# Strided mask and identity in one first transfer, fewer warm-up products, masks put by ScalarE, merged mix_t, strided sums behind the adds, and u^T's transfers on SyncE: a fused sparse-attention and low-rank/channel mixer kernel

## The chip, the cores and the metric

The kernel runs on one core of a Trainium2 chip. The core has five engines that work side by side, each through its own list of instructions in order: TensorE (PE in the profile; PEld is its weight load), VectorE (DVE), ScalarE (ACT), GpSimd (POOL) and SyncE (SP, which here only issues DMAs). They wait for one another by semaphores. Sixteen DMA engines move data between the main memory (HBM) and the on-chip memory (SBUF); TensorE writes its sums into a small memory of eight banks (PSUM). The metric is the device time of one execution in microseconds (us).

## What is computed

Attention over 8 batches, 8 heads, 576 positions and 64 channels, with two kinds of masks, and then a mixer. Cut to what matters:

```python
# q, k, v: (8, 8, 576, 64)
scores = np.matmul(q, k.transpose(0, 1, 3, 2)) / 8
pos = np.arange(576); rel = pos[:, None] - pos[None, :]
mask_local = (rel >= 0) & (rel < 32)                       # heads 0 to 3
mask_strided = (rel >= 0) & (pos[None, :] % 32 == pos[:, None] % 32)   # heads 4 to 7
attn = softmax(np.where(mask, scores, -1e9)) @ v
x = attn.transpose(0, 2, 1, 3).reshape(8, 576, 512)
h = x.transpose(0, 2, 1) @ U @ V                           # U (576, 32), V (32, 576): mixes positions
u = x + h.transpose(0, 2, 1)
out = u + np.maximum(u @ w_ch1, 0) @ w_ch2                 # w_ch1 (512, 2048), w_ch2 (2048, 512)
```

U, V and the two weight matrices come as 64-bit floats, and are converted on the chip. Products that must be exact are made of a high and a low part (`uh` and `ul`, `gh` and `gl`, two parts of each weight), three products in place of one.

## The kernel before, in words

**Blocks.** The channel mixer runs in nine blocks n = 0 to 8: one for the first 512 positions of each batch, and a last one for the eight tails of 64 positions. A block goes through 16 chunks `fc` of 128 hidden units. `gemm1` (line 648) makes 12 products of 128x512 for a chunk, ScalarE makes `gh` from it (line 652), VectorE `gl` (line 653), and `gemm2` (line 665) adds 12 more products into four banks `acc`. gemm2 runs one chunk behind gemm1. At a block's end `split` (lines 637 to 640) makes the next block's `uh` (ScalarE) and `ul` (VectorE) from `raw`, the transposed u, and `finish` (line 672) adds `acc` to u and stores it; the next block's gemm2 waits for these adds, since it writes the same banks.

**Attention beside it.** While block n runs, the attention of batch n + 1 is put between its products, a step at a time: `advance` hands out the steps of `attention` by half chunks ("slots", 32 a block) at rates that A_EARLY, A_LATE and A_TAIL give. For batches 2 to 7: the two pairs of local heads (`local_pairs`: scores, softmax, transposes, outputs), then the strided heads' results are copied in, `mix_t` makes x^T U in two halves of 256 channels (lines 514 and 518), `mix_u` adds V's product (lines 537 and 539), `mix_tail` does the 64 positions at the end, and `transposes` turns u by VectorE (line 619) and by 32 small DMAs into `raw` (line 624), half of them issued by ScalarE and half by SyncE. The strided heads of these batches are not done on TensorE: GpSimd multiplies (lines 442 and 470) and VectorE sums (lines 444 and 472), at a rate that S0 and S1 set by slots.

**The prefix.** The batches 0 and 1 are done at the start, all eight pairs of heads (`early_pair`, in the order 2, 3, 0, 1 of the pairs of each batch: strided pairs first). Their positions are sorted so that the strided mask becomes a band as the local one is. `quarter` then makes u^T of batch 0, a quarter of the channels for each pair. Scores begin with two products that put the mask into PSUM (line 340: an identity times the mask), on which the products of q and k are added (line 346); then maximum and difference (VectorE, lines 356 and 357), exponential (ScalarE, line 361), transposes (line 368, with the identity `ident`), a copy (line 371) and the outputs (line 381). In front of the first and of the second scores stand eight products of zeros each (line 338, WARM), to keep TensorE busy. SyncE loads q, k and v first, then weights; GpSimd issues the strided mask, the local mask with the 16-bit identity, and `ident`.

**Weights.** In block 0 the weights are still being converted (lines 129 to 132, 205 and 206: ScalarE and VectorE), each load gated by a one-word copy on GpSimd (line 169) behind a due exponential.

**Order.** A scheduler sets each engine's list from the order in which the code is written, readiness by its own estimate, and hints `issue_after`. `psx2` gives the two banks `px` (in the prefix `acc` as well), one user at a time.

## Time and profile before

| what | value |
|---|---|
| median of 3 runs (lowest, highest) | 927.82 us (927.54, 929.11) |
| the profiled execution's own time | 928.37 us |
| its span, first to last instruction | 926.1 us |
| mean granted TensorE clock | 0.991 |
| HBM read, written | 54.14 MB, 11.67 MB |
| DMA packets | 39036, 75.29 MB |

The page cuts the span into 40 slices of 23 us, with one digit per slice: the busy share in tenths (9 is 90% or more), and for the clock the tenths of full speed that TensorE was granted.

```profile
PE   7899989999999999999999999999999999999997
DVE  4579996665886588658765786667863341122111
POOL 1223493343853393429433764356530000000000
PEclk9899999999999999999999999999999999999999
DMA  9869313201230125011500141014200230001001
```

VectorE's digits are high in the third to sixth slice, which is block 0, and the DMA's in the first three. POOL's work ends with the strided heads of batch 7.

### The profile page before, as it was taken

The page shows a single profiled execution, that of the slowest core. Times are in us where ns is not written, and L with a number is a line of the kernel's source. Part 1 is how long each engine was busy: PE and PEld are TensorE (multiplying, and loading weights), DVE is VectorE, ACT ScalarE, POOL GpSimd, SP SyncE. Part 2 cuts the span into 40 slices and gives each one's busy share as a digit, 9 for nine tenths or more (in the row PEclk, how much of TensorE's full clock was granted, in tenths as well). Part 3 has the DMA queues.
Part 4 walks back from the last instruction along what each step waited for, and adds up shares of the span by engine and source line. Part 5 has one row for each costly group of instructions (what it writes and reads, how often), then busy time and mean ns, then how long its engine had stood idle before and what let it go on. Part 6 is the DMA issues. An engine that isn't in the chain of part 4 may idle for free.

```text
span 926.1 us, 16819 instructions
## 1 busy us (share of the span) xinstructions
PE 902.6 (97%) x6997; PEld 718.0 (78%) x6998; DVE 548.6 (59%) x895; ACT 244.2 (26%) x478; POOL 338.4 (37%) x378
## 2 busy tenths in 40 slices
PE   7899989999999999999999999999999999999997
PEld 4667767777887788778877787778877888888885
DVE  4579996665886588658765786667863341122111
ACT  3457522142123312331224121422142111121110
POOL 1223493343853393429433764356530000000000
PEclk9899999999999999999999999999999999999999
DMA  9869313201230125011500141014200230001001
GB/s 352 299 205 357 117 54 107 73 2 52 76 145 2 52 55 178 1 52 33 181 8 18 50 168 50 1 53 148 73 1 1 57 120 17 1 1 46 0 1 46
DMA packets 39036, 75.29 MB, mean 81 GB/s; under 512 B 6464, under 2 KB 22864, under 8 KB 37040
## 3 DMA queue, kind: packets, MB, share of 16 engines
q1 hardware_dynamic: 27312, 66.87, 20.7%
q10 hardware_dynamic: 10560, 4.73, 2.0%
q0 software_dynamic: 1088, 2.62, 0.8%
q8 instruction: 55, 0.90, 0.4%
q14 instruction: 21, 0.17, 0.1%
HBM read 54.14 MB, written 11.67 MB: 71 GB/s over the span
## 4 chain that ended last, share of the span: by engine, by line
PE 84%; DVE 4%; DMA 2%; POOL 1%; issue 1%; ACT 0%; SPq 0%; DVEq 0%; ACTq 0%; POOLq 0%
PE acc L665 40%; PE ph L648 39%; PE px L381 1%; DMA w<-in_w_dram 1%; PE px L346 1%; DVE cv L132 1%; DVE s_st L444 1%; PE px L368 1%; PE px L514 1%; DMA od<-x 1%; PE px L537 1%; DMA st<-in_strided_dram 1%; DVE w L206 1%; POOL tmp L442 1%; DVE gl L653 0%
## 5 line engine op out<-in xcount | busy, mean ns | idle before, releaser
L653 DVE SCALAR_TENSOR_TENSOR gl<-ph,gh 128x512 fp32r<-128x512 f32 x144 | 98.9, 688 | 230.1 <-ACT gh L652 229.4
L648 PE MATMUL ph<-uh,w 128*128 128x512 f32 x648 | 215.9, 394 | 0.0
L652 ACT ACTIVATE gh<-ph 128x512 fp32r<-128x512 f32 x144 | 86.2, 599 | 476.9 <-PE ph L648 400.8
L470 POOL TENSOR_TENSOR tmp<-st,s_st 128x448 f32<-128x448 f32 (+7 forms) x162 | 137.3, 876 | 190.8 <-DVE st L472 106.8
L442 POOL TENSOR_TENSOR tmp<-st 128x576 f32<-128x576 f32 (+6 forms) x162 | 175.0, 1121 | 76.5 <-DMA st<-in_strided_dram 66.6
L665 PE MATMUL acc<-w,gh 128*128 128x512 f32 x648 | 196.8, 391 | 0.0
L648 PEld LDWEIGHTS ph<-uh,w 128*128 128x128 f32 x648 | 121.9, 189 | 26.8
L665 PEld LDWEIGHTS acc<-w,gh 128*128 128x128 f32 x648 | 121.3, 188 | 25.6
L472 DVE TENSOR_REDUCE st<-tmp 128x64 f32<-128x64 f32 (+8 forms) x162 | 136.3, 878 | 7.8 <-POOL tmp L470 7.0
L648 PE MATMUL ph<-ul,w 128*128 128x512 f32 x324 | 126.8, 391 | 0.0
L665 PE MATMUL acc<-w,gl 128*128 128x512 f32 x324 | 121.6, 392 | 4.1 <-DVE gl L653 4.1
L444 DVE TENSOR_REDUCE s_st<-tmp 128x9 f32<-128x576 f32 (+6 forms) x162 | 87.2, 563 | 17.5 <-POOL tmp L442 16.7
L665 PEld LDWEIGHTS acc<-w,gl 128*128 128x128 f32 x324 | 61.0, 188 | 18.4 <-DVE gl L653 5.2
L648 PEld LDWEIGHTS ph<-ul,w 128*128 128x128 f32 x324 | 61.1, 189 | 12.6
L487 ACT COPY xg<-st 32x256 f32<-32x256 f32 x96 | 38.8, 404 | 9.1 <-DVE st L472 7.7
L525 DVE TENSOR_TENSOR ta<-px,ta 32x256 f32<-32x256 f32 x42 | 17.6, 420 | 36.5 <-ACT ta L523 35.6
L672 DVE TENSOR_TENSOR xg<-acc,xg 128x512 f32<-128x512 f32 x36 | 22.9, 682 | 13.4 <-PE acc L665 13.4
L539 DVE TENSOR_TENSOR xg<-px,xg 128x512 f32<-128x512 f32 x28 | 18.0, 684 | 11.9 <-PE px L537 11.9
L648 PE MATMUL ph<-uh,w6a 128*128 128x512 f32 x72 | 24.3, 398 | 0.0
L640 DVE TENSOR_TENSOR ul<-raw,uh 128x512 fp32r<-128x512 f32 x32 | 21.1, 682 | 5.3 <-ACT uh L639 5.3
L648 PE MATMUL ph<-uh,w1a 128*128 128x512 f32 x72 | 23.9, 391 | 0.0
L648 PE MATMUL ph<-uh,w2a 128*128 128x512 f32 x72 | 23.9, 391 | 0.0
(265 smaller groups left out, 1252.9 us busy)
## 6 DMA issues: line engine op xcount, KB each, us to landing
w<-in_w_dram SPq DMA_DIRECT2D x9, 1024.0 KB, 13.3
out_dram<-xg SPq DMA_DIRECT2D x32, 256.0 KB, 2.1
v<-in_pairs_dram SPq DMA_DIRECT2D x12, 585.0 KB, 5.1
st<-in_strided_dram SPq DMA_DIRECT2D x6, 1152.0 KB, 5.4
qk<-in_pairs_dram SPq DMA_DIRECT2D x12, 576.0 KB, 5.1
late<-in_pairs_dram SPq DMA_DIRECT2D x8, 585.0 KB, 8.3
late<-in_pairs_dram SPq DMA_DIRECT2D x8, 576.0 KB, 8.1
raw<-bt SPq DMA_DIRECT2D x128, 32.0 KB, 1.9
```

The lines of the kernel that those rows point to most:

```text
L442: nc.gpsimd.tensor_tensor(out=tmp[:, 0:n], in0=sk[:, j0:j0 + n], in1=sq[:, i:i + 1].broadcast_to([128, n, D]), op=ALU.mult)
L444: late.append(lambda tmp=tmp, n=n, i=i, j0=j0: nc.vector.tensor_reduce(out=s_st[:, i, j0:j0 + n], in_=tmp[:, 0:n], axis=AX.X, op=ALU.add))
L470: nc.gpsimd.tensor_tensor(out=tv, in0=sv[:, 0:i + 1, d0:d0 + step], in1=s_st[:, i, 0:i + 1].broadcast_to([128, i + 1, step]), op=ALU.mult)
L472: late.append(lambda tv=tv, i=i, d0=d0, step=step: nc.vector.tensor_reduce(out=o_st[:, i, d0:d0 + step], in_=tv.rearrange("p j d -> p d j" ...
L487: nc.scalar.copy(out=xg[32 * i4:32 * i4 + 32, :, cs], in_=o_st[rows, i4:16:4, :])
L539: nc.vector.tensor_tensor(out=xg[:, t + s, :], in0=pv[:, s, :], in1=xg[:, t + s, :], op=ALU.add)
L640: nc.vector.tensor_tensor(out=lo, in0=raw[:, :, :, dc, :], in1=hi.bitcast(F32), op=ALU.subtract)
L648: nc.tensor.matmul(ph, w_parts[fc, 0][:, part, 128 * dc:128 * dc + 128], ut[:, dc, :], start=(dc == dcs[0] and i == 0), stop=(dc == dcs[-1 ...
L652: marks.setdefault("gh", []).append(nc.scalar.activation(out=gh, in_=ph, func=AF.Relu).ins)
L653: low = nc.vector.scalar_tensor_tensor(out=gl, in0=ph, scalar=0.0, in1=gh.bitcast(F32), op0=ALU.max, op1=ALU.subtract)
L665: last = nc.tensor.matmul(accs[n][s // 2][:, s % 2, :], gt[:, cs], w_parts[fc, 1][:, part, :], start=(fc == 0 and i == 0 and n > 0), stop= ...
L672: nc.vector.tensor_tensor(out=ot, in0=accs[n][s // 2][:, s % 2, :], in1=ot, op=ALU.add)
```

## The change

What it does, part by part:

- **Loads.** The masks lie in another order in memory; the strided one with the 16-bit identity is one transfer of 112 KB, and it is the first that SyncE issues. `ident` and the local mask are issued by ScalarE instead of GpSimd.
- **Warm-up.** Three products in place of eight ahead of the second scores.
- **Masks.** For batches 2 to 7, `masked` lets ScalarE copy the local mask into PSUM, one step ahead of the scores, and the two mask products go. The scores are put behind the last product of the gemm1 written before them.
- **Outputs.** In `outputs` only the first products clear what the bank held (`start`), and the others are put behind them.
- **mix_t** is done once for 512 channels instead of twice for 256, after the strided copies.
- **Strided sums** are put behind the adds of the last `finish` by a hint, and at the end of a block `finish` comes ahead of the attention steps of that half chunk.
- **u^T.** All 32 small DMAs of a block are issued by SyncE, and `raw` is laid out so that each of their rows is 1 KB in one piece on both sides; `split` takes 128x256 in eight steps instead of 128x512 in four.
- The rates follow: N_EARLY, A_LATE and S1.

```diff
-N_EARLY = 20
-N_LATE = 48
+N_EARLY = 17
+N_LATE = 47
...
-A_LATE = (1, 28, N_LATE)
+A_LATE = (2, 26, N_LATE)
...
-S1 = (14, 14)
+S1 = (12, 12)
...
-WARM = {0: 8, 1: 8}
+WARM = {0: 8, 1: 3}
...
-    raw = const.tile([128, 4, 4, NDC, 32], F32, name="raw")
+    raw = const.tile([128, 2, 4, 2, NDC, 32], F32, name="raw")
...
+    def masked():
+        sp = psx2()
+        nc.scalar.copy(out=sp[:, :, 0:320], in_=mask_l.broadcast_to([128, 320, 2]).rearrange("p x h -> p h x"))
+        return sp
+
+    def scores(kT, qT, mask, sp=None):
+        if sp is None:
+            sp = psx2()
+            with_mask(sp, mask)
...
-                    last = nc.tensor.matmul(op[32 * o4:32 * o4 + 32, hh, (D + 1) * t:(D + 1) * t + D + 1],
-                                            PT[rows, 32 * c:32 * c + 32], vt[rows, c], start=True, stop=True,
+            with tc.issue_after(first) if t else nullcontext():
...
+                        last = nc.tensor.matmul(op[32 * o4:32 * o4 + 32, hh, (D + 1) * t:(D + 1) * t + D + 1],
+                                                PT[rows, 32 * c:32 * c + 32], vt[rows, c], start=t == 0, stop=True,
...
-            sp = scores(kT, qT, mask_l)
+            sp = masked()
+            yield
+            with tc.issue_after(marks["ph"][-1]):
+                sp = scores(kT, qT, mask_l, sp)
...
+    def reduced(**what):
+        with tc.issue_after(marks["out"][-1]) if "out" in marks else nullcontext():
+            nc.vector.tensor_reduce(**what)
...
-    def mix_t(b, half):
+    def mix_t(b):
...
-        ps_a = psx1()[:, 0:256]
+        ps_a = psx1()
...
-        far_dma(out=mask_s, in_=masks[:, 448:768])
-        far_dma(out=masks_sb, in_=masks[:, 0:448])
-        far_dma(out=ident, in_=eye)
+        dma(out=mask_first, in_=masks[:, 0:448])
+        od_dma(out=ident, in_=eye)
+        od_dma(out=mask_l, in_=masks[:, 448:768])
...
-            yield from mix_t(b, 0)
             yield "strided"
             yield from strided_copies(b)
-            yield from mix_t(b, 1)
+            yield from mix_t(b)
...
-                    (od_dma if q % 2 else dma)(out=raw[32 * q:32 * q + 32, t:t + 2, a].rearrange("p s d x -> p s (d x)"),
-                                               in_=bt[32 * a:32 * a + 32, q].rearrange("p s d x -> p s (d x)"))
+                    dma(out=raw[32 * q:32 * q + 32, t // 2, a].rearrange("p s d x -> p (s d x)"),
+                        in_=bt[32 * a:32 * a + 32, q].rearrange("p s d x -> p (s d x)"))
...
-            hi, lo = (u[:, dc, :].rearrange("p (s a x) -> p s a x", s=4, a=4) for u in (uh, ul))
+            for t in range(2):
+                hi, lo = (u[:, dc, 256 * t:256 * t + 256].rearrange("p (s a x) -> p a s x", s=2, a=4) for u in (uh, ul))
...
-        advance(2 * step)
+        ends = len(pend) > 1 and pend[0][1] == NFC - 1
+        if not ends:
+            advance(2 * step)
...
-            item = pend.pop(0)
-            gemm2(*item)
-            if item[1] == NFC - 1:
-                finish(item[0])
+            gemm2(*pend.pop(0))
+        if ends:
+            finish(n - 1)
+            advance(2 * step)
```

How the scheduler puts it, at three places. Names are tiles (`late` and `early` hold the prefix's q, k, v and intermediates, `px` and `acc` are PSUM).

TensorE in the prefix, from the second scores to the first pair's outputs (before: line 340 masks, 346 scores, 368 transposes, 381 outputs), first before:

```order
L340 MATMUL px<-early,masks_sb 128x320
L346 MATMUL px<-late 32x32 x2
L346 MATMUL px<-late 32x64 x9
L368 MATMUL acc<-ident,late 128x128 x4
L368 MATMUL acc<-ident,late 128x64
L346 MATMUL px<-late 32x64 x25
L381 MATMUL acc<-late 32x65 x40
```

and now (338 masks, 357 scores, 379 transposes, 397 outputs):

```order
L338 MATMUL px<-early 128x320
L357 MATMUL px<-late 32x32 x2
L357 MATMUL px<-late 32x64 x23
L379 MATMUL acc<-ident,late 128x128 x4
L379 MATMUL acc<-ident,late 128x64
L357 MATMUL px<-late 32x64 x11
L397 MATMUL acc<-late 32x65 x40
```

The first pair's transposes stand behind 25 of the second pair's 36 scores instead of behind 11, with five warm-up products less ahead of them.

VectorE in block 0, between its eleventh and its twelfth `gl` (131, 132 and 206 are weight conversions, 444 strided sums), first before:

```order
L653 SCALAR_TENSOR_TENSOR gl<-ph,gh 128x512
L444 TENSOR_REDUCE s_st<-tmp 128x4
L131 TENSOR_SCALAR cv<-cv 128x1024
L444 TENSOR_REDUCE s_st<-tmp 128x9
L444 TENSOR_REDUCE s_st<-tmp 128x5
L552 TENSOR_TENSOR xt<-px,xt 64x512
L444 TENSOR_REDUCE s_st<-tmp 128x9
L206 TENSOR_TENSOR w_1587<-cv,w_1587 128x2x512
L132 SCALAR_TENSOR_TENSOR cv<-w_1629,cv 128x1024
L653 SCALAR_TENSOR_TENSOR gl<-ph,gh 128x512
```

and now (445 strided sums, 638 transposes of u):

```order
L674 SCALAR_TENSOR_TENSOR gl<-ph,gh 128x512
L445 TENSOR_REDUCE s_st<-tmp 128x3
L445 TENSOR_REDUCE s_st<-tmp 128x9
L638 STREAM_TRANSPOSE bt<-xg 128x4x4x32 x2
L131 TENSOR_SCALAR cv<-cv 128x1024
L445 TENSOR_REDUCE s_st<-tmp 128x4
L206 TENSOR_TENSOR w_1567<-cv,w_1567 128x2x512
L674 SCALAR_TENSOR_TENSOR gl<-ph,gh 128x512
```

In all there are 17 strided sums ahead of the twelfth `gl` where there were 20, the last conversion's line 132 stands behind it, and four transposes of u are ahead of it where there were two.

VectorE at a block boundary (the one at 257.40 us before), from the `gl` of the last chunk but one, first before (453 to 461 the strided softmax, 640 split, 472 strided sums, 672 the adds of finish):

```order
L653 SCALAR_TENSOR_TENSOR gl<-ph,gh 128x512 x2
L458 TENSOR_REDUCE m_st<-s_st 128x18
L640 TENSOR_TENSOR ul<-raw,uh 128x512
L459 TENSOR_SCALAR m_st<-m_st 128x18
L640 TENSOR_TENSOR ul<-raw,uh 128x512 x2
L460 RECIPROCAL m_st<-m_st 128x18
L640 TENSOR_TENSOR ul<-raw,uh 128x512
L461 TENSOR_TENSOR s_st<-s_st,m_st 128x324
L472 TENSOR_REDUCE st<-tmp 128x64 x3
L672 TENSOR_TENSOR xg<-acc,xg 128x512 x2
```

and now (483 to 486 the softmax, 660 split, 693 the adds, 445 the sums):

```order
L483 TENSOR_REDUCE m_st<-s_st 128x18
L660 TENSOR_TENSOR ul<-raw,uh 128x4x2x32
L484 TENSOR_SCALAR m_st<-m_st 128x18
L485 RECIPROCAL m_st<-m_st 128x18
L660 TENSOR_TENSOR ul<-raw,uh 128x4x2x32
L486 TENSOR_TENSOR s_st<-s_st,m_st 128x324
L660 TENSOR_TENSOR ul<-raw,uh 128x4x2x32
L674 SCALAR_TENSOR_TENSOR gl<-ph,gh 128x512
L660 TENSOR_TENSOR ul<-raw,uh 128x4x2x32 x5
L693 TENSOR_TENSOR xg<-acc,xg 128x512 x4
L445 TENSOR_REDUCE st<-tmp 128x64 x7
L674 SCALAR_TENSOR_TENSOR gl<-ph,gh 128x512
```

The last chunk's `gl` stood ahead of split and now stands behind three of its eight pieces; the four adds come in one run ahead of the strided sums. ScalarE's list at this place likewise has three pieces of split ahead of the last chunk's `gh` and five behind it, where `gh` stood ahead of all four.

More of the change, by code (lines that the diff above doesn't have):

```diff
@@ L330, in od_reads, with with_mask @@
             far_dma(out=xt[tb + 32 * i4:tb + 32 * i4 + 32, 256:512], in_=ov[16 + i4])
-    def scores(kT, qT, mask):
-        sp = psx2()
+    def with_mask(sp, mask):
         done = marks.setdefault("scores", [])
@@ L607, in attention @@
             yield from mix_tail(0)
-            for half in range(2):
-                yield from mix_t(b, half)
+            yield from mix_t(b)
             yield from mix_u(b)
@@ L647, in gemm1 @@
             for i, (part, ut) in enumerate(((0, uh), (0, ul), (1, uh))):
[L648 to L649 removed]
+                last = nc.tensor.matmul(ph, w_parts[fc, 0][:, part, 128 * dc:128 * dc + 128], ut[:, dc, :],
+                                        start=(dc == dcs[0] and i == 0), stop=(dc == dcs[-1] and i == 2))
+        marks.setdefault("ph", []).append(last.ins)
         gh = mp.tile([128, 512], F32R, name="gh", bufs=2)
@@ L677, in finish @@
                 dma(out=out[n, 128 * s:128 * s + 128, :], in_=ot)
+        marks.setdefault("out", []).append(last.ins)
     conv = weights()
```

56 lines of the change are left out of this document (27 added, 29 removed).

## The prediction

> **What bounds the kernel now.** I cut the span by block (a block is one pass over the 16 weight chunks for one batch of tokens, and begins with its first product of line 648), then asked who ended TensorE's waits, and last read the rows around the places that the diff touches. The windows give length, busy time of PE, PEld, DVE, ACT and POOL (instructions), then the granted clock, the DMA share and GB/s:
>
> ```profile
> 0.00:49.51 49.51, 39.00 (x967) 26.73 (x968) 24.95 (x48) 20.21 (x40) 9.64 (x23) 0.90 0.90 321
> 49.51:159.17 109.66, 103.12 (x863) 79.20 (x858) 96.56 (x154) 50.22 (x73) 52.63 (x58) 0.98 0.48 170
> 257.40:355.82 98.42, 98.42 (x745) 78.69 (x744) 69.64 (x117) 25.44 (x55) 51.05 (x55) 1.00 0.22 74
> 744.99:829.76 84.77, 84.77 (x375) 70.19 (x374) 18.47 (x28) 11.95 (x20) 0.00 (x0) 1.00 0.13 38
> ```
>
> So there are three regimes. Up to 49.51 us (the prefix, attention of two batches) TensorE is busy for 39.00 of 49.51 us beside DMAs at 0.90. In block 0 VectorE is busy 96.56 of 109.66 us. In the two later rows TensorE is never idle: a block with attention takes 98.42 us and one without 84.77, so only TensorE's own small products lie between them, and what is taken out there comes off the time.
>
> **The prefix.** The costliest of TensorE's waits in the whole span (total, times, longest; it falls in block 0), and the rows of the start in order of time (start, length, what; in brackets the idle time and its end):
>
> ```profile
> PE acc L665 <- DVE gl L653: 4.1, 3, 1.9
> ```
> ```profile
> 0.74 2.65 SPq L96 DMA_DIRECT2D late<-in_pairs_dram  x5
> 1.26 3.60 PE L338 MATMUL acc<-raw 128*128 128x512 bf16 x8 [1.26 <-DVE raw L115]
> 7.75 0.45 PE L340 MATMUL acc<-early,masks_sb 128*128 128x320 bf16 x2 [2.89 <-DMA masks_sb<-in_masks_dram]
> 8.12 0.92 PE L346 MATMUL acc<-late 64*32 64x32 f32 x72
> 9.37 3.16 PE L338 MATMUL px<-raw 128*128 128x512 bf16 x7 [0.33 <-issue]
> 10.79 0.74 ACT L361 ACTIVATE late<-late 128x640 f32<-128x640 f32 x1 [8.77 <-DVE late L357]
> 13.08 0.86 PE L368 MATMUL acc<-ident,late 128*128 128x128 f32 x5
> 14.67 0.76 PE L381 MATMUL acc<-late 64*32 64x65 f32 x53
> 16.31 0.45 PE L381 MATMUL acc<-late 64*32 64x65 f32 x27 [0.89 <-issue]
> 22.54 1.03 PE L381 MATMUL acc<-late 64*32 64x65 f32 x79 [0.77 <-issue]
> 28.38 0.34 PE L381 MATMUL px<-late 64*32 64x65 f32 x13 [1.89 <-issue]
> ```
> ```profile
> masks_sb<-in_masks_dram POOLq DMA_DIRECT2D x1, 112.0 KB, 5.7
> DMA to landing us min/median/max: 3.8/3.8/3.8
> ```
>
> The second line is that of the first k and q, SyncE's first issue at 0.74 us: they were there at 4.5. The mask and identity, which GpSimd issues, took 5.7 us and released TensorE at 7.75 only. With the mask ahead of them in SyncE's queue, its 112 KB put k and q back by one issue and a quarter of a us: I take 5.2 us for the first scores, after the warm-ups that end at 4.86. Gain there 8.12 - 5.2 = 2.9 us (bounds: 0 if the transfer is no faster in SyncE's queue, 3.3 if only the warm-ups set the start). Behind it, the first exponential ends at 11.53, but its transposes start at 13.08, because the eight warm-ups and the second scores stand ahead of them. Five warm-ups of 0.43 us less are 2.1 us, of which 13.08 - 11.53 = 1.55 lay on this path. Together the first outputs (14.67) come 4.4 us earlier.
>
> What is late next: three products of line 381 start after idle time that no semaphore ended, while TensorE consumed some 250 instructions between each two of them. The queue view of 12 to 30 us has three packets for code:
>
> ```profile
> q8 instruction: 3, 0.05, 1.1%
> ```
>
> that is 16 KB each, one per stall, so TensorE waits for its own program behind a full DMA. I take it that a block of code is asked for when the one before it is entered, since one packet goes out per stall; then these stalls move with the second scores, and I let 0.4 us get lost. The term is **-4.0 us** (0 if this queue paces the stage whatever comes earlier, -6 if the stalls shrink). In the Trainium skill, "Runtime: NRT & Kernel Launch", section "Instruction fetch mechanics", the code comes in 16 KiB pages of 256 instructions and that is called mostly hidden. The trace agrees with the size and not with the hiding: 0.89, 0.77 and 1.89 us stood open.
>
> **Block 0.** Here VectorE decides: from 105 to 140 us it is busy 33.81 of 35 us, and each of TensorE's three waits for gl falls there.
>
> ```profile
> 105.00:140.00 35.00, 30.87 (x126) 23.97 (x125) 33.81 (x47) 11.03 (x14) 31.65 (x25) 0.95 0.14 40
> L132 DVE SCALAR_TENSOR_TENSOR cv<-w,cv 128x1024 int32<-128x1024 int32 x4 | 7.2, 1796 | 0.0
> L444 DVE TENSOR_REDUCE s_st<-tmp 128x9 f32<-128x576 f32 x7 | 5.1, 741 | 0.0
> ```
> ```profile
> L640 DVE TENSOR_TENSOR ul<-raw,uh 128x512 fp32r<-128x512 f32 x4 | 2.6, 670 | 0.0
> ```
>
> By the order of the changed program, ahead of the twelfth gl stand three strided sums less (2.2 us), one weight conversion less (1.8) and two block transposes of 128x512 more (taken at the 0.67 of line 640's shape, 1.3): **-2.7 us**, which TensorE can give back from its 4.1 us of waits and the clock of 0.95 behind them. Bounds 0 and -5. The shift of the prefix goes through, since weights are requested behind the same exponentials.
>
> **Steady blocks.** The mask products, and one half of mix_t, each between products of 128x512:
>
> ```profile
> 345.10 0.39 PE L648 MATMUL ph<-uh,w 128*128 128x512 f32 x1
> 345.32 0.45 PE L340 MATMUL px<-masks_sb 128*128 128x320 bf16 x2
> 345.50 0.96 PE L665 MATMUL acc<-w,gh 128*128 128x512 f32 x3
> ```
> ```profile
> 307.51 0.39 PE L648 MATMUL ph<-ul,w 128*128 128x512 f32 x1
> 307.83 0.64 PE L514 MATMUL px<-xg,U_sb 128*32 128x256 f32 x8
> ...
> 308.64 0.73 PE L648 MATMUL ph<-uh,w 128*128 128x512 f32 x2
> ```
> ```profile
> L514 PE MATMUL px<-xg,U_sb 128*32 128x256 f32 x8 | 0.6, 391 | 0.0
> L371 ACT COPY PT<-px 128x576 f32<-128x576 f32 x2 | 1.3, 641 | 3.1 <-PE px L368 3.1
> ```
>
> Large products start 0.23 us apart (84.77 / 375). Masks: 345.50 - 345.10 - 0.23 = 0.17, and the three products behind take 0.96 instead of 0.39 + 2 x 0.23 = 0.85, so 0.28 in all, for 12 pairs less the one in block 0 where TensorE waits anyway: **-3.1 us**. ScalarE's copies that take their place are priced by the copy of 128x576, 0.64 x 640/576 = 0.71 us each; they lie on an engine that is busy 25.44 of 98.42 us, and by the order 34 large products (7.8 us) stand between the outputs that free the buffer and the scores that want it masked. That cover gone, each would cost its 0.71, in all 8.5 us.
>
> Half of mix_t: 308.64 - 307.51 - 0.23 = 0.90, and 0.11 behind it (0.73 for two instead of 0.62): 1.01. The merged one has half the switches but streams the same columns: one wave of four products takes 0.64 - 0.39 = 0.25 for 256 columns (the whole group less one product), and there are two waves, so 0.50 comes on top, and a quarter of that for the rows of the tail, of 64 columns: 1.01 + 0.6 = 1.6 against 2.02, **-0.4 us** in each of six blocks (bounds 0 and -1), -2.4. In block 0 it is hidden by VectorE.
>
> The scores of batch 2's first pair stood in five pieces and now stand in one; I leave that unpriced, as a gain of under 1 us.
>
> **At the block boundaries** the change adds work. Rows around the boundary at 257.40 (transposes, issues, split, and time from issue to landing):
>
> ```profile
> 235.17 0.70 DVE L619 STREAM_TRANSPOSE bt<-xg 128x512 f32<-128x512 f32 x1
> ...
> 240.91 0.70 DVE L619 STREAM_TRANSPOSE bt<-xg 128x512 f32<-128x512 f32 x1
> ```
> ```profile
> 246.51 1.25 ACTq L99 DMA_DIRECT2D raw<-bt  x2
> ...
> 251.83 0.38 SPq L96 DMA_DIRECT2D qk<-in_pairs_dram  x1
> ...
> 254.83 2.17 ACT L639 CAST uh<-raw 128x512 fp32r<-128x512 f32 x4
> ```
> ```profile
> raw<-bt SPq DMA_DIRECT2D x128, 32.0 KB, 1.9
> ```
>
> The first pair of transposes ends at 235.9 and the second at 241.6, the last issue of raw at 247.8, split begins at 254.8; one of these transfers lands 1.9 us after its issue. The 16 issues a half block, shared by two queues, become 16 on SyncE alone. Now one takes 0.62 us (1.25 / 2) with its rows in two parts; in one part it is of the plain kind of line 96, which took 0.38 for 128 rows. At 0.38, 32 of them last 12.2 us instead of two queues' 16 x 0.62 = 9.9, so from 235.9 they end at 248.1 instead of 247.8, over six us ahead of split: nothing for it. At 0.62 this cover is gone, which is rival 5. What queues behind them on SyncE are the loads of the next heads, wanted in the next block.
>
> Split itself has eight narrow steps on ScalarE and on VectorE instead of four wide ones. A narrow one lies between 0.34 (half of line 640's 0.67) and 0.67; I take 0.42, since 0.74 for 576 elements (line 444) says that length makes most of the cost. That is 0.7 us more on VectorE, and the gl of the block's last chunk now stands behind three of them. TensorE wants it 2.7 + 0.9 us after split begins (twelve and four products at 0.23); I reckon it ready at 3.3: four short steps of the softmax sums (1.4 by their lengths at line 444's rate), three narrow ones (1.3) and itself (0.67, a 128x512 as well). So thin a margin is missed sometimes: **+1.4 us**, 0.2 at each of seven boundaries (0 to +7).
>
> Sum: -4.0 - 2.7 - 3.1 - 2.4 + 1.4 = -10.8 us. The profiled execution took 928.37 us (2.3 outside its span), the median of the three runs is 927.82; so 917.6 on the one, and **917.0 us** for the median.
>
> **The rivals.** (1) The prefix is paced by its full DMA, and nothing earlier helps. The 0.90 share up to 49.51 speaks for it; against it, that the wait for the mask stood alone in front of everything. Then 921.0; chance 0.22. (2) VectorE's stage in block 0 and the prefix both shrink to their bounds (-2.3 and -2 more): 912.7; 0.15. (3) With fewer warm-ups the clock stays halved longer.
>
> ```profile
> 5.53:8.94 3.41, 1.20 (x74) 1.00 1.04 420
> 8.94:12.36 3.42, 3.09 (x16) 0.50 1.07 345
> 22.60:26.00 3.40, 2.52 (x106) 1.00 1.04 414
> ```
>
> (Length, PE busy, clock, DMA share.) After 1.20 us of work in 3.41 the next stretch had half the clock; a stretch with 2.52 of 3.40 had full clock and kept it over the next, in which it fell idle. The changed kernel has about 2.7 us of work in the first stretch (scores, three warm-ups, masks, scores), so I expect it spared; if not, two half-speed stretches cost up to 3.4 us: 920.4, chance 0.07. The Trainium skill, "TensorE: Matmul & The Clock Gate", section "What's actually happening", has this as a rule, with free-running windows of 3413 ns, which speaks against taking warm-ups out; the stretches above agree with its length. (4) The change does not do what it says: prefix and block 0 stay as they are, since DMA and VectorE pace them, and the boundaries cost their +7: 927.8 - 5.5 + 7 = 929.3; 0.03. (5) Slower: U^T's issues on SyncE take 0.62 as now. From 235.9 on 32 of them last 19.8 us, to 255.7, and the last lands at 257.6. Then come two of ScalarE's pieces of split and, behind them by the order, the last chunk's gh: ready at 257.6 + 0.7 + 0.6 = 258.9, wanted by TensorE 2.7 us after split begins, at 257.5. That is 1.4 us of waiting, and if the clock falls as in block 0 (0.95 over 35 us is 1.75 us lost, half of one 3.41 us stretch) 1.7 more. Seven times 3.1 are 22: 917.0 + 22 = 939. It turns the sign from 1.6 us a boundary (10.8 / 7), and the clock decides it. That a contiguous row costs as much as a divided one is unlikely by line 96's 0.38: 0.05. My own case, 913 to 920, keeps 0.48.
>
> A measurement of this kernel tells about 0.2% (1.9 us) from no change. Faster by more than that: 0.48 + 0.22 + 0.15 + 0.07 = 0.92; within it 0.03; slower 0.05. The range takes in (1) to (3) and the bounds around them: 910.0 to 923.5.
>
> **What would show it.** No mask wait and first scores near 5.2 us; first outputs near 10.3; the first product of the weights near 45.5 instead of 49.51; the wait for gl in block 0 down by some two us; steady blocks at 97.4 us or below, without idle TensorE; and at block starts few waits for gl. I am wrong if the first weight product still starts after 48 us, or if TensorE shows waits of over half a us at each block's start.

## The result, and the profile after

The changed kernel takes **918.70 us** (median of 4 runs, 915.96 to 922.49) against 928.47 (4 runs, 927.54 to 930.70). The ratio is 0.9894, with a 95% interval from 0.9854 to 0.9935. The prediction was 917.0 us, 910.0 to 923.5. So the total came out as forecast, but two of its terms did not, in opposite directions. The profiled execution took 918.27 us (span 916.5). One more run of the kernel before, of 1144.96 us at a mean clock of 0.731, enters no figure here.

The windows of the kernel after, for the prefix, block 0, a block with attention and one without (length; busy time of PE, PEld, DVE, ACT, POOL; granted clock, DMA share, GB/s):

```profile
0.00:52.31 52.31, 40.14 (x967) 28.64 (x967) 27.94 (x54) 21.91 (x42) 7.85 (x22) 0.87 0.88 315
52.31:154.49 102.18, 97.36 (x798) 76.85 (x797) 92.98 (x145) 48.59 (x73) 49.90 (x54) 1.00 0.49 177
253.47:349.68 96.21, 96.21 (x720) 77.33 (x719) 67.82 (x113) 27.05 (x58) 50.26 (x53) 1.00 0.19 62
736.00:820.32 84.32, 84.32 (x373) 69.82 (x372) 18.23 (x31) 12.21 (x24) 0.00 (x0) 1.00 0.12 38
```

The first weight product comes at 52.31 us, not at 45.5: it was 49.51, so the prefix got longer by this mark (about 1 us of that is the sixth pair's five transposes, which moved ahead of it). Block 0 fell from 109.66 to 102.18, and block 1 starts 4.68 us earlier. Blocks 1 to 7 together fell from 670.59 to 665.83 us (-4.76). The last block takes 96.34 us before and 96.18 after, with TensorE busy for 89.92 in both. Of the steady blocks, 2 to 6 take 96.2 to 96.9 us after, below the predicted 97.4, and block 1 does not, as the rows before and after show:

```profile
159.17:257.40 98.23, 98.23 (x706) 78.04 (x705) 65.62 (x108) 25.40 (x55) 49.19 (x52) 1.00 0.18 58
154.49:253.47 98.98, 98.98 (x733) 79.53 (x731) 68.20 (x115) 27.18 (x58) 51.40 (x56) 1.00 0.17 54
```

It grew because it took over work: 38 products for scores of batch 2's first pair ran in block 0 before and run in block 1 now.

What TensorE waited for, in the kernel after (total, times, longest):

```profile
PE acc L686 <- DVE gl L674: 2.9, 2, 1.8
PE acc L295 <- DVE tst L293: 2.8, 3, 1.5
PE acc L684 <- DVE xt L415: 1.9, 1, 1.9
PE acc L397 <- issue: 1.6, 1, 1.6
...
PE px L357 <- issue: 1.4, 1, 1.4
...
PE acc L686 <- ACT gh L673: 0.6, 2, 0.3
```

The wait for the mask (2.9 us) is gone, the waits for gl fell from 4.1 to 2.9. New are two waits of 0.3 us for gh, 5.9 us after the starts of blocks 3 and 5, and, in the prefix, the waits of line 295 for `tst` (2.8 and 0.4 us). This is TensorE in the prefix after (start, length; in brackets the idle time and its end):

```profile
6.01 0.92 PE L357 MATMUL acc<-late 64*32 64x32 f32 x72 [0.92 <-DMA late<-in_pairs_dram]
...
9.48 0.86 PE L379 MATMUL acc<-ident,late 128*128 128x128 f32 x5 [0.87 <-ACT late L372]
...
11.06 0.81 PE L397 MATMUL acc<-late 64*32 64x65 f32 x58 [0.38 <-ACT late L382]
13.46 0.42 PE L397 MATMUL acc<-late 64*32 64x65 f32 x22 [1.58 <-issue]
...
24.79 0.50 PE L295 MATMUL acc<-xt,tst 96*128 96x512 f32 x1 [1.50 <-DVE tst L293]
```

The first outputs start at 11.06 instead of 14.67, so 3.6 us of the predicted 4.4 were there. They were gone at the third pair's exponential. ScalarE's rows show where (the exponentials are line 372, the 64-bit conversions line 129):

```profile
13.82 0.50 ACT L129 ACTIVATE early<-xg 128x320 f32<-128x320 f32 x1 [2.81 <-DMA xg<-in_U_dram]
14.21 0.73 ACT L372 ACTIVATE late<-late 128x640 f32<-128x640 f32 x1
...
20.51 0.66 ACT L129 ACTIVATE cv<-w0a 128x512 f32<-128x512 f32 x1 [1.62 <-DMA w0a<-in_w_dram]
...
22.46 0.73 ACT L372 ACTIVATE late<-late 128x640 f32<-128x640 f32 x1
```

ScalarE works its list in order. Ahead of the second exponential stands U's conversion, which waits for a transfer; ahead of the third stands that of the first weight. The kernel before has the same order, with U's conversion at 14.51 us and the first weight's at 20.14 (361 are the exponentials):

```profile
16.36 0.74 ACT L361 ACTIVATE late<-late 128x640 f32<-128x640 f32 x1 [1.34 <-DVE late L357]
...
22.08 0.74 ACT L361 ACTIVATE late<-late 128x640 f32<-128x640 f32 x1
```

So the second exponential comes 2.15 us earlier and the third 0.38 us later. The fourth to sixth, at 29.77, 38.23 and 47.87 us, are 2.2, 2.5 and 2.1 earlier again, but TensorE gains nothing from that: it begins the fifth pair's transposes at 41.82 us, where it was at 41.84 before.

And the clock. Two pairs of windows after (same columns as above): a window with little TensorE work, and the stretch at half clock behind it:

```profile
11.49:14.90 3.41, 1.36 (x57) 0.73 (x50) 1.45 (x4) 1.08 (x3) 0.00 (x0) 1.00 1.02 304
14.90:21.73 6.83, 6.22 (x90) 5.08 (x91) 5.50 (x11) 4.31 (x9) 1.49 (x2) 0.50 1.03 413
...
42.21:45.62 3.41, 1.71 (x75) 0.98 (x73) 1.54 (x4) 1.26 (x3) 0.00 (x0) 1.00 0.95 280
45.62:49.04 3.42, 3.35 (x16) 2.82 (x17) 2.68 (x4) 0.74 (x2) 0.38 (x2) 0.50 0.75 304
```

With a third stretch at 35.38 the prefix has 13.65 us recorded at half clock, against 10.24 before. Block 0 has none, against 3.41. In these two executions the whole 2.8 us by which the first weight product is late arise from 41.8 us on: line 357 waits 1.42 us without a semaphore ("issue" in the list above), the last of these stretches at half clock makes 1.7, the sixth pair's transposes 0.8 and two short waits 0.6, less a wait of 1.3 for `xg` that is gone (3.2 in all, so 0.4 too much).

In the steady blocks, the merged mix_t between large products:

```profile
308.52 0.39 PE L668 MATMUL ph<-uh,w 128*128 128x512 f32 x1
308.84 1.06 PE L536 MATMUL px<-xg,U_sb 128*32 128x512 f32 x8
309.83 0.42 PE L540 MATMUL px<-xt,U_sb 64*32 64x128 f32 x8
310.19 0.73 PE L686 MATMUL acc<-w,gh 128*128 128x512 f32 x2
```

It costs 310.19 - 308.52 - 0.23 = 1.44, and 0.11 behind it, so 1.55 us against 2.02 for two halves.

Last, the 32 issues of u^T for one block, which SyncE now makes alone:

```profile
228.08 20.16 SPq L96 DMA_DIRECT2D raw<-bt  x32
```

That is 0.63 us each (20.16 / 32). They did not get cheaper in rows of 1 KB.

### The profile page after: what moved, and what is told of

Same layout as the page of the kernel before. It is cut to its first block, busy times and chain, and to the rows that moved or that the text cites. A ratio compares the mean times of both kernels' runs of the same rounds, so it can differ in the third digit from the quotient of the medians.

```text
span 916.5 us, 16576 instructions
## 1 busy us (share of the span) xinstructions
PE 892.7 (97%) x6857; PEld 715.3 (78%) x6857; DVE 547.5 (60%) x899; ACT 253.1 (28%) x501; POOL 336.0 (37%) x375
## 4 chain that ended last, share of the span: by engine, by line
PE 89%; DVE 2%; ACT 0%; issue 0%; DVEq 0%; ACTq 0%
PE acc L686 42%; PE ph L668 41%; PE px L397 1%; PE px L357 1%; PE px L379 1%; PE px L536 1%; PE px L558 1%; DVE s_st L445 0%; DVE w L206 0%; PE px L540 0%; DVE cv L132 0%; DVE xg L693 0%; DVE cv L131 0%; PE px L567 0%; DVE xg L560 0%; ACT gh L673 0%
## 5 line engine op out<-in xcount | busy, mean ns | idle before, releaser
L467 POOL TENSOR_TENSOR tmp<-st 128x576 f32<-128x576 f32 (+6 forms) x162 | 177.1, 1130 | 128.1 <-DMA st<-in_strided_dram 70.8
L660 DVE TENSOR_TENSOR ul<-raw,uh 128x256 fp32r<-128x256 f32 x64 | 24.4, 418 | 12.7 <-ACT uh L659 9.7
L659 ACT CAST uh<-raw 128x256 fp32r<-128x256 f32 x64 | 23.2, 404 | 18.9 <-PE ph L668 11.2
L668 PE MATMUL ph<-uh,w0a 128*128 128x512 f32 x72 | 24.2, 391 | 0.0
L668 PE MATMUL ph<-uh,w3a 128*128 128x512 f32 x72 | 23.8, 391 | 0.0
```

Source lines behind the costliest of these rows:

```text
L467: nc.gpsimd.tensor_tensor(out=tmp[:, 0:n], in0=sk[:, j0:j0 + n], in1=sq[:, i:i + 1].broadcast_to([128, n, D]), op=ALU.mult)
L659: nc.scalar.copy(out=hi, in_=raw[:, t, :, :, dc, :])
L660: nc.vector.tensor_tensor(out=lo, in0=raw[:, t, :, :, dc, :], in1=hi.bitcast(F32), op=ALU.subtract)
L668: last = nc.tensor.matmul(ph, w_parts[fc, 0][:, part, 128 * dc:128 * dc + 128], ut[:, dc, :], start=(dc == dcs[0] and i == 0), stop=(dc == ...
```

## The experiments

The table sums up the profiled executions. "Half clock" is the time recorded at 0.50 up to the end of block 0. The record of the clock does not begin with the trace, though. Its first entry, "record from", says full clock in all fourteen, and ahead of it TensorE ran at half clock: warm-up products of 128x512 start 0.43 us apart there, as they do under a recorded 0.50, and 0.22 apart under a recorded 1.00. In e4 the record begins at 13.88 us only. Its second group of eight warm-ups, and then three of the changed kernel, 2 us behind the start of its record:

```profile
9.73 3.59 PE L338 MATMUL px<-raw 128*128 128x512 bf16 x8
```
```profile
6.87 0.82 PE L336 MATMUL px<-raw 128*128 128x512 bf16 x3
```

"Corrected" is the end of block 0 less half of the half clock, since such a product takes twice the time there; the first figure goes by the record, the second counts the start as half clock too. In a part of that start TensorE only waited for data, so the second takes off too much: what only one of the two shows is not shown. The two columns on the right are means over all timed runs of a kernel: the granted clock, and the span times that clock. For the kernel before there are 48 such runs (median 929.34 us). The mean clock of a profiled execution counts the start as full clock (half of it is 2.0 to 6.9 us); the other runs have no trace that would tell.

| kernel | median us | first weight product | block 0 ends | half clock | record from | corrected | blocks 1-7 | clock | span x clock |
|---|---|---|---|---|---|---|---|---|---|
| before | 929.34 | 49.51 | 159.17 | 13.65 | 5.53 | 152.3, 149.6 | 670.59 | 0.9925 | 919.7 |
| after | 918.70 | 52.31 | 154.49 | 13.65 | 4.67 | 147.7, 145.3 | 665.83 | 0.9885 | 906.6 |
| e1, eight warm-ups | 919.45 | 52.86 | 156.85 | 20.48 | 4.33 | 146.6, 144.4 | 665.91 | 0.9894 | 908.3 |
| e2, early mask alone | 931.82 | 54.62 | 164.88 | 27.31 | 4.21 | 151.2, 149.1 | 670.80 | 0.9860 | 916.9 |
| e3, ScalarE's masks alone | 930.96 | 48.02 | 157.00 | 10.24 | 4.54 | 151.9, 149.6 | 675.51 | 0.9929 | 922.6 |
| e4, merged mix_t alone | 921.15 | 47.23 | 153.07 | 3.41 | 13.88 | 151.4, 144.4 | 668.66 | 0.9945 | 914.3 |
| f1, line 295 later | 918.12 | 45.35 | 157.67 | 20.48 | 6.53 | 147.4, 144.2 | 665.91 | 0.9907 | 907.9 |
| f2, mask late again | 917.50 | 50.07 | 153.83 | 10.24 | 9.51 | 148.7, 144.0 | 665.82 | 0.9922 | 908.4 |
| f3, pace 1 to 28 | 933.62 | 50.79 | 154.54 | 17.07 | 6.91 | 146.0, 142.6 | 681.14 | 0.9890 | 921.8 |
| f4, sums free | 924.87 | 50.52 | 157.38 | 20.48 | 6.42 | 147.1, 143.9 | 671.17 | 0.9871 | 911.1 |
| g1, ScalarE's list | 917.03 | 48.60 | 153.30 | 17.07 | 4.45 | 144.8, 142.5 | 665.78 | 0.9896 | 905.7 |
| g2, U and V earlier | 918.42 | 51.34 | 156.03 | 20.48 | 7.25 | 145.8, 142.2 | 665.97 | 0.9885 | 906.2 |
| h1, fillers | 917.32 | 51.84 | 153.94 | 13.65 | 5.05 | 147.1, 144.6 | 665.93 | 0.9922 | 908.5 |
| h2, list and mask late | 922.39 | 45.49 | 158.89 | 20.48 | 3.92 | 148.6, 146.7 | 665.75 | 0.9900 | 911.5 |

(f1 and h2 list some 160 small products behind the first weight product that the others have ahead of it; only the end of block 0 compares there. Each row is one execution, and these differ: before, e3 and e4 have the same instructions ahead of the first weight product and reach it at 49.51, 48.02 and 47.23, and after, f3 and f4 at 52.31, 50.79 and 50.52. So the changed prefix is the later one, by some 3 us in the mean, and a difference of 2 us between two rows says nothing.)

**e1: eight second warm-ups again.** `WARM = {0: 8, 1: 3}` became `{0: 8, 1: 8}` in the changed kernel.

> The changed kernel with eight warm-up products ahead of the second scores again instead of three. Disputed: why the first weight product came at 52.31 us and not at 45.5. Theory C (clock): fewer warm-ups and idle windows halve the clock, 13.7 us of the prefix at 0.50 against 6.8 before; then the half-clock time falls to 7 us or less and the first weight product comes near 49 us (-3.4), the whole 915.3 us. Theory D (code and DMA): TensorE is paced by its code blocks, which come behind a full DMA; then the first weight product stays at 52 to 53 us, whatever the clock does, and the time at 918.7 within 0.2%. Theory O (order): the new list order makes TensorE wait for VectorE's tst; then it moves by the waits at line 295 (3.0 us together now), which I cannot say in advance.

Ratio 0.9913 (0.9898 to 0.9927). The half-clock time did not fall, the first weight product stayed at 52.86. (The 6.8 us that the expectation gives for the prefix before are 10.24 by its record.) So it was not the fewer warm-ups that cost the clock, and taking them out is no loss.

**e2: the prefix's part alone, in the kernel before.**

```diff
-        far_dma(out=mask_s, in_=masks[:, 448:768])
-        far_dma(out=masks_sb, in_=masks[:, 0:448])
-        far_dma(out=ident, in_=eye)
+        dma(out=mask_first, in_=masks[:, 0:448])
+        od_dma(out=ident, in_=eye)
+        od_dma(out=mask_l, in_=masks[:, 448:768])
-WARM = {0: 8, 1: 8}
+WARM = {0: 8, 1: 3}
```

> The kernel before with the prefix's part of the change alone: strided mask and identity first on SyncE, the local mask and the identity in float by ScalarE, three second warm-ups. The prediction's term alone: first scores 5.2 to 6.0 us instead of 8.12, first weight product 45.5 instead of 49.51, 924.5 us instead of 928.5. Theory D (code and DMA pace the stage): first weight product 49 to 50, 928.5. Theory C (clock): half-clock time over 10 us in the prefix, first weight product 50 or later, 929 or more. Theory O (order: what lost the lead is the other parts' reordering): 45.5 to 47.

Ratio 1.0043 (1.0028 to 1.0058): **slower** by 3.2 us by the medians, where the prediction's term said 4 us faster. Its windows for the prefix and block 0:

```profile
0.00:54.62 54.62, 42.49 (x967) 29.74 (x967) 27.94 (x54) 21.88 (x42) 7.74 (x22) 0.81 0.88 321
54.62:164.88 110.26, 103.23 (x851) 79.67 (x851) 96.05 (x148) 47.65 (x71) 49.90 (x57) 0.97 0.44 154
```

The granted clock is 0.81 in the prefix (0.90 before). Over all its runs the mean clock is 0.0065 lower than before, while span times clock is 2.8 us less. Read so, the early mask saves some work time and loses more by the clock; that is argued from these two means, with the unrecorded start in them, and no run shows it by itself.

**e3: ScalarE's masks alone, in the kernel before.** Lines as in the diff (`masked`, and `scores` behind the last gemm1). It leaves out the change to `outputs`, so that local scores may replace the copied mask instead of adding to it; number and size of the instructions are what the part needs. N_LATE is 50 instead of 48.

> The kernel before with ScalarE's mask copies in the local pairs alone (12 pairs of mask products gone; the scores stand behind the last gemm1). The prediction's term: 11 x 0.28 = 3.1 us less, 925.4 us instead of 928.5, each steady block with attention 0.56 us shorter, and TensorE never waiting for the copies. Rival: the copies are not covered, 0.71 us each, 8.5 us back: 934. Rival: scatter of the schedule in block 0 and at the boundaries (+-2 us) hides it: 927 to 930.

Ratio 1.0032 (1.0016 to 1.0047), slower. The copies are not waited for, but TensorE's first line of waits reads now:

```profile
PE acc L680 <- DVE gl L668: 8.7, 5, 3.2
```

Two of the five are new, ahead of the changes to blocks 2 and 6 (1.5 and 0.9 us), and the longest, in block 0, was 1.3 before. Blocks 1 to 7 take 4.9 us more. The first rival (the copies uncovered) is out. Alone, the part brings waits for gl, and its scores stand in 23 pieces behind block 0 (13 before, 12 in the changed kernel), so what the mask products took does not come free; this does not add up to all of the 4.9.

**e4: the merged mix_t alone, in the kernel before** (with the counts of steps N_EARLY 17 and N_LATE 45 that go with it).

> The kernel before with mix_t merged into one alone. The prediction's term: 0.4 us in each of six blocks, 926.1 us instead of 928.5; by the changed kernel's trace (1.56 against 2.06 us an instance) 0.50 each, 925.5. If the merged VectorE steps (128x512 instead of 128x256) come late for mix_u or make gl wait: blocks longer than 98.3 us and TensorE waiting for tst or gl, 928.5 or more.

Ratio 0.9927 (0.9911 to 0.9942): 7 us, three times the term. Blocks 1 to 7 give 1.9 of them, as priced (2.4). The rest lies up to the end of block 0. The first weight product comes 2.3 us earlier behind the same instructions, which is no more than executions differ. Block 0 takes 105.84 us instead of 109.66. Of these 3.8 us the half clock of 3.41 us, which is gone, makes 1.7, shorter waits for gl 0.7 (3.4 for 4.1), the merged products 0.4, and about 0.8 is only moved: 36 of the 38 score products of batch 2's first pair run in block 1. So the merged mix_t reaches far beyond its own products, by what it moves in VectorE's and TensorE's lists. Whether the clock had a part up to block 0 the table can't say, as 13.88 of the first 47.23 us of e4 are not recorded.

**f1: line 295 behind the next pair's outputs.** `quarter` yields ahead of its last products, and these get `issue_after(marks["PV"][-1])`.

> The changed kernel, in whose prefix the product of line 295 (and the copies of u behind it) is listed behind the next pair's outputs, as it stood in the kernel before; everything else as changed, three warm-ups and the early mask too. Theory O (order: the early mask made the scheduler list line 295 among the outputs, where TensorE waits in order for VectorE's tst, 3.3 us in four waits of the changed kernel, and the clock falls behind such waits): the waits at line 295 go, the half-clock time falls below 13.7 us, the first weight product comes at 46 to 49 us instead of 52.31 and the time is 913 to 916. Theory D (DMA or VectorE paces the stage whatever TensorE's order): other waits take their place, first weight product 51 to 53, 918.7 within 0.2%.

Ratio 0.9881 (0.9860 to 0.9902), no different from the change itself. The waits at line 295 went from 3.2 to 0.7 us, but time that no semaphore ends came instead:

```profile
PE acc L399 <- issue: 5.0, 3, 2.3
...
PE px L359 <- issue: 0.9, 1, 0.9
...
PE acc L297 <- DVE tst L293: 0.7, 1, 0.7
```

Such stalls were 3.0 us in the changed kernel. Theory O falls as the cause: what the list no longer waits for, it waits for without a semaphore. I read these stalls as waits for code. In the changed kernel the two of them end 1.5 and 1.3 us after a packet of 16 KB on the queue for code has come in (at 11.93 and 44.37 us).

**f2: the mask late again, eight second warm-ups, all else as changed** (the three loads of e2's diff the other way round).

> The changed kernel with the prefix's part undone alone: the mask and identity loads on GpSimd again, eight second warm-ups, so the wait for the mask of 2.9 us is back. If that part really costs time (its run by itself was 3.2 us slower than the kernel before): first weight product 48 to 50 us instead of 52.31, 914 to 916. If the early mask gains and other parts of the change made the prefix late: first weight product 55 or later, 921 or more.

Ratio 0.9874 (0.9857 to 0.9891). Without the prefix's part the kernel is as fast as with it; the intervals overlap. Whether it does more or less work up to the end of block 0 stays open: by the record its corrected end is 1.0 us later, and with its start of 9.51 us counted 1.3 earlier.

**f3: the old pace.** `A_LATE = (2, 26, N_LATE)` became `(1, 28, N_LATE)`.

> The changed kernel with the steady blocks' list spread over half-slots 1 to 28 as before instead of 2 to 26, so that U^T's transposes and their 32 issues come two half-slots, 6.0 us, later. Theory U (an issue costs 0.63 us on SyncE whatever the row, 20.1 us for 32, and only the earlier place covers it: last landed 249.49, split done 251.46, wanted 253.5): TensorE waits about 4 us for ul or gh at each of six or seven boundaries, 24 to 28 us in all, about 944. If the issues start so early that two half-slots do not matter: no wait over 0.5 us at boundaries, 918.7 to 921.

Ratio 1.0048 (1.0030 to 1.0067); blocks 1 to 7 take 15.3 us more than in the changed kernel. SyncE's row and TensorE's waits:

```profile
231.90 20.18 SPq L96 DMA_DIRECT2D raw<-bt  x32
```
```profile
PE ph L668 <- DVE ul L660: 5.6, 6, 1.5
...
PE ph L668 <- ACT uh L659: 1.5, 3, 1.1
```

The issues end at 252.08, when the next block wants its first `uh` at 254.3. So theory U is right in kind: TensorE waits for `ul` or `uh` at the start of each of blocks 2 to 7. These waits are 7.1 us and not 24 to 28, since the issues came 3.8 us later and not 6.0. The rest of the 15.3 is not theirs; the old pace also lets the scores stand in 22 pieces behind block 0 instead of 12, which costs some 3.7 us between the large products.

**f4: the strided sums without their rule** (`reduced` no longer stands behind the adds of `finish`).

> The changed kernel without the rule that puts the strided sums behind the block's closing adds. In the kernel before with ScalarE's masks alone TensorE waited for gl at every second block start, 3.0 us in all. If that rule is what keeps gl in time: gl waits at block starts, 3 to 6 us more, 922 to 925. If it is the merged mix_t or the changed pace that does: no such waits, 918.7 within 0.2%.

Ratio 0.9952 (0.9932 to 0.9972), 6 us slower than the change. The size is as expected, the place is not: block 1 alone has it (104.26 us instead of 98.98), where gemm2 waits for the adds, and not for gl, and the clock falls behind the wait (0.50 from 170.26 to 173.67 us):

```profile
PE acc L686 <- DVE xg L693: 2.2, 2, 1.8
```

**g1: ScalarE's list.** U's conversion got `issue_after(marks["exp"][1])` instead of `marks["PT"][0]`, and the early weights stand behind `marks["exp"][min(7, i + 2)]` instead of `marks["less"][...]`.

> The changed kernel with ScalarE's list of the prefix altered: the conversion of U (line 129) stands behind the second exponential instead of ahead of it, and that of each early weight behind the exponential of the third and later pairs. In the changed kernel the second exponential stood behind U, which landed at 13.80 us (idle 2.81 us, exponential at 14.21, its input there at 12.45), and the third behind the first weight, which landed at 20.49 (idle 1.62, exponential at 22.46, input there at 20.5). Theory D1 (the full DMA paces the prefix through ScalarE's order): second exponential starts near 12.5, third near 20.5 or earlier, first weight product 1.5 to 3.5 us earlier (49 to 51 us), 915 to 917. Theory D2 (the code blocks behind the full DMA pace TensorE anyway): the exponentials come earlier, but stalls that no semaphore ends grow by as much: first weight product 52, 918.7 within 0.2%. Theory O: the waits at line 295 stay and decide, 918.7.

Ratio 0.9873 (0.9851 to 0.9894). ScalarE's rows:

```profile
11.84 0.74 ACT L372 ACTIVATE late<-late 128x640 f32<-128x640 f32 x1 [1.47 <-DVE late L368]
13.65 0.49 ACT L129 ACTIVATE early<-xg 128x320 f32<-128x320 f32 x1 [1.07 <-DMA xg<-in_U_dram]
...
19.68 0.74 ACT L372 ACTIVATE late<-late 128x640 f32<-128x640 f32 x1
20.33 0.65 ACT L129 ACTIVATE cv<-w0a 128x512 f32<-128x512 f32 x1
```

The second and third exponentials come 2.4 and 2.8 us earlier and the first weight product 3.7 (1.8 against the earliest of the three executions with the changed prefix), as theory D1 said. U and the first weight land only 0.2 and 0.6 us earlier than in the changed kernel. At the end of block 0 1.2 us are left, with 17.07 us of half clock instead of 13.65. The time is not shown to be lower.

**g2: U and V requested two loads earlier**, and the early weights as in g1.

> The changed kernel with U and V requested behind the first three loads of heads instead of behind five, and the early weights' conversions behind the exponentials of the third and later pairs as in the run beside it; ScalarE's list keeps U's conversion ahead of the second exponential. TensorE's list is that of the changed kernel. Theory D1: U lands near 11 us instead of 13.80, the second exponential starts near 12.5 and VectorE's small-weight steps ahead of the third maximum end earlier too, third exponential at 19 to 20.5, first weight product 2 to 4 us earlier (48 to 50), 914.5 to 917. Theory D2 (code blocks): 52 and 918.7 within 0.2%.

Ratio 0.9885 (0.9865 to 0.9904). The exponentials come at 12.30 and 19.71 as expected, but the first weight product only at 51.34, within the range of the changed prefix, with 13.65 us of half clock recorded ahead of it. So early exponentials alone do not bring the first weight product forward: the fifth starts at 37.97, almost where the changed kernel has it (38.23), and at 36.25 in g1. No gain is seen in the time.

**h1: fillers.** To g1 were added products of zeros:

```diff
+            with tc.issue_after(marks["exp"][-1]):
+                for _ in range(2):
+                    nc.tensor.matmul(pp[:, 0:512], zeros[:, 0:128], zeros[:, 128:640], start=True, ...)
...
+        with tc.issue_after(hi_t):
+            for _ in range(3):
+                nc.tensor.matmul(ph[:, 128:512], zeros[:, 0:128], zeros[:, 128:512], start=True, ...)
```

> The run with ScalarE's list altered, and besides 23 products of zeros on TensorE in the prefix (two of 128x512 ahead of seven of the eight pairs' transposes, three of 128x384 ahead of three pairs' products of line 295), listed where TensorE waited. In the ten traces so far the end of block 0 minus half of the half-clock time up to there lies at 151.2 to 152.3 us for the four kernels without the merged-and-changed list of block 0, and at 144.8 to 148.7 for the other eight. Theory C (waits in the prefix halve the clock, and each us of half clock costs half a us): the half-clock time up to the end of block 0 falls from 17.1 us in the run without fillers to 7 or less, worth 5; the fillers cost 23 x 0.22 = 5.1 us less what falls into the waits (over half), so block 0 ends at 149 to 152 us instead of 153.3 and the time is 913 to 916. Rival theory (DMA and code pace the prefix and the half clock is only a sign of it): the half-clock time falls, but block 0 ends at 153 to 156, 917 to 920.

(The traces meant are those of the ten runs and of the two kernels themselves, twelve.) Ratio 0.9876 (0.9855 to 0.9898), no different from g1. It missed as a test: the half-clock time went from 17.07 to 13.65 us only, and the stalls that I read as waits for code grew:

```profile
PE acc L405 <- issue: 1.8, 1, 1.8
PE px L405 <- issue: 1.7, 1, 1.7
```

With two more, of 1.0 and 0.7, they are 5.2 us in all, against 1.7 in g1.

**h2: g1's list with the mask late.**

> The changed kernel with ScalarE's list altered as in the run with ScalarE's list, and with the mask loads on GpSimd and eight second warm-ups again. Theory C: half-clock time up to the end of block 0 about 10 us as in the run with the mask late, ScalarE's list gains 1 to 2 us as it did with the early mask, block 0 ends at 151 to 153 us, 914.5 to 917. Theory that the early mask itself gains 2.9 us once the list is mended: 2 to 3 us slower than the run with ScalarE's list, 919 to 920.

Ratio 0.9933 (0.9915 to 0.9950), slower than either theory said: 20.48 us of half clock, not 10. It is 4.9 us slower than f2, so ScalarE's new list gains nothing while the mask is late. Why it is slower stays open: corrected, block 0 ends where f2 has it by the record and 2.7 us later with the start counted, and of the 4.9 us the mean clock (0.9900 for 0.9922) makes 2.0 at most, while span times clock is 3.1 higher.

No version is shown to beat the change: f2, g1 and h1 lie 1.2 to 1.7 us below it by their medians, within the intervals.

## Why the prediction was right, and where it was wrong

**Prefix, -4.0: wrong.** By the prediction's own sign (a first weight product behind 48 us) this term failed. The chain up to the first outputs was right (11.06 for 10.3), though k and q, behind the mask, landed at 5.97 us instead of 4.54, so that the first scores came at 6.01 and not at 5.2. The code moved along, as I took it: its first packet came in at 11.93 instead of 15.05. The step that failed is "these stalls move with the second scores, and I let 0.4 us get lost": I followed the lead for two pairs and then let it run on to the first weight product. It ended at the next transfers. DMA is full up to 30 us in both kernels, before and after:

```profile
21.00:30.00 9.00, 5.46 (x221) 3.96 (x219) 4.71 (x10) 5.74 (x13) 1.62 (x4) 0.97 1.02 408
21.00:30.00 9.00, 7.16 (x187) 5.58 (x186) 5.67 (x11) 5.15 (x13) 1.62 (x4) 0.96 1.04 405
```

U lands 1.2 us later than before (13.80 for 12.61), and through ScalarE's order the second and third exponentials stand behind U and the first weight, whatever TensorE did before. That much is shown by g1 and g2: both mend it, and the third exponential comes at 19.7 us. It is rival 1, which had 0.22. That the first weight product is late for this reason alone is not shown, since g1 brings it forward and g2 does not; by 41.8 us TensorE was level with the kernel before, and the rest came from a stall and the clock. The clock is rival 3's price without its cause: half clock not from fewer warm-ups (e1), but from windows in which TensorE works too little. Alone, the part costs 3 to 4 us (e2); within the change it brings nothing that the runs can tell (f2).

**Block 0, -2.7: too small.** It became 7.5 us shorter, 6.4 without the five transposes that moved. The waits for gl fell from 4.7 to 3.2 us by the gaps between products (predicted: two us less), the half clock of 3.41 us went (1.7), and so did a stall without a semaphore of 1.4 us; the merged mix_t is 0.5, and the wait for xt grew by 0.8. Another 1.1 us are only moved: that is what the 38 score products, which now run in block 1, took between the large products. About one us stays unassigned. The step that failed here is "In block 0 it is hidden by VectorE": the merged mix_t alone shortens block 0 by 3.8 us (e4), half of the gain. Prefix and block 0 together gave 4.7 of the predicted 6.7 us.

**Steady blocks: right.** Masks, mix_t and boundaries were to give -3.1 - 2.4 + 1.4 = -4.1, with under 1 us of scores unpriced; they gave -4.76. I sorted this by what lies between the large products: the scores with their masks take 2.5 us less, although 38 more of them run here, the mix_t products 2.2 less, the two waits for gh make 0.9 more, and 1.0 less lies among the large products themselves. A merged mix_t saves 0.47 us (0.4 predicted). The masks' term is right only in the whole change: alone it comes with more pieces of scores and with waits for gl (e3).

**Boundaries, +1.4: near in size (0.9), on a wrong premise.** I took 0.38 us for an issue in one part; it is 0.63, as rival 5 had it, which I called unlikely. What I overlooked is that the new pace puts the transposes earlier: I left the first pair's end at 235.9 us, but the issues start at 228.08 and the last has landed before `split` needs it. f3 takes that away and gives rival 5's waits, of 7.1 us in all instead of 22. The cover is some 5 us from the last issue (248.2) to the next block's first product (253.47).

**The sum.** In the profiled executions the first weight product is 2.8 us later, where 4.0 earlier was forecast, block 0 is 7.5 shorter instead of 2.7, and blocks 1 to 7 are 4.8 shorter instead of 4.1: 9.4 us for 10.8. So the total was right by cancellation, a lucky one: the prefix lost what it was to gain, and block 0 gave more than twice its term. How much of this is work and how much is clock stays open. By span times clock the change saves 919.7 - 906.6 = 13.1 us. The mean clock fell by 0.0040, which is 3.7 us if every half-clocked us counts, and 2.4 by the 48 runs of the kernel before, in which 0.001 of clock goes with 0.59 us. That would be more work saved up to the end of block 0 than I reckoned, and less kept. The profiled pair does not show it (corrected, block 0 ends 4.6 or 4.3 us earlier, and 6.7 were forecast), and the unrecorded start is in these means. That the half clock costs this is a relation over all these runs; changing the clock alone was tried (h1) and did not succeed, so it is not shown by itself.

## What to carry to other kernels

An earlier start is worth what is left of it behind the next two or three transfers: follow it through each engine's list, not only through the engine that waited. After a change, read the granted clock window by window, and look where its record begins before you compare kernels by span times clock; here a stage of short waits seems to have lost by the clock what it had saved (e2). The parts of this change had no prices of their own: the masks, which cost 2 to 3 us alone, and the mix_t, which alone gave three times its term, show that. Test parts by taking each out of the whole, not only by putting each in alone.

## What the runs showed of the hardware

**The clock follows a share, not a pause.** I cut the first 170 us of all fourteen traces into windows of 3.413 us on the clock's own grid, from the first record on. Of those at full clock, every one with under 1.63 us of TensorE work was followed by half clock, none with over 2.22 us, and of those between, some. Out of a recorded half-clocked window the clock came back only where TensorE had been busy at least 3.08 of 3.41 us, and not behind all of these (before: 3.41 us of work from 29.42 on, and half clock again). That is no threshold: the unrecorded start of f2 ended behind a window with 2.55 us. In the Trainium skill, "TensorE: Matmul & The Clock Gate", section "HAM oscillation — how this bites in real kernels" gives the rule as no idle gaps over about 3.4 us. The rows above are stricter: 1.71 us of work in 3.41, with no gap over 1.42 us, was followed by half clock.

**The clock's record begins late.** In all fourteen traces its first entry says full clock and stands at 3.9 to 13.9 us, and the warm-up products ahead of it run at the pace of half clock (0.43 us apart for 0.22). A mean clock over the span counts that start as full.

**A stall without a semaphore does not go away with the work ahead of it.** In the changed kernel, f1, g1 and h1 TensorE lost 3.0, 5.9, 1.7 and 5.2 us to idle time that no semaphore ended (rows over half a us), with much the same program. That it waits for its code there is read from the packets of 16 KB that came in 1.3 and 1.5 us before the changed kernel's two stalls ended.

**An SBUF to SBUF transfer of 32 rows costs SyncE 0.63 us to issue** in rows of two 512-byte parts (three in 1.88 us in the kernel before; 0.62 on ScalarE's queue) and in whole rows of 1 KB alike (32 in 20.16 us).
